# Two early pairs of layer 2, W_in's squares on GpSimd, and a new order table

## The chip, the cores and the metric

The kernel runs on one core of a Trainium2 chip. TensorE (PE in the rows) multiplies matrices into PSUM; VectorE (DVE), ScalarE (ACT) and GpSimd (POOL) do elementwise work; SyncE (SP) issues most of the DMAs between HBM and SBUF. Each engine runs its own list of instructions in order and waits for the others on semaphores. The metric is the time of one execution on the device, in microseconds (us). Of the kernel before, three runs are shown.

## The reference

Three parts follow one another: attention with rotary positions, a first feed-forward layer with a gate, and a second one with a rational activation. The 2304 tokens are 4 batches of 576.

```python
q_rot, k_rot = rotate(q), rotate(k)                      # 4 batches, 8 heads, 576 positions, 64 wide
scores = (1 / sqrt(64)) * q_rot @ k_rot^T
attn = exp(scores - max(scores))
attn = attn / (sum(attn) + 1e-09)
x = (attn @ v).transpose(0, 2, 1, 3).reshape(2304, 512)

h = x @ moe_w_in                                          # 512 -> 2048, layer 1
x = (h * clip(h + 3, 0, 6) / 6) @ moe_w_out               # 2048 -> 512

h = x @ moe2_w_in                                         # 512 -> 2048, layer 2
P = a0 + a1*h + a2*h^2 + a3*h^3
Q = 1 + |b0|*|h| + |b1|*h^2
out = (P / (Q + 1e-06)) @ moe2_w_out                      # 2048 -> 512
```

## The kernel before

All products run in 16 bit: a 32-bit matrix is scaled by a power of two and split into a high and a low half, and three matmuls (high by high, high by low, low by high) make one product. So every operand costs elementwise work: a copy to 16 bit for the high half, and a subtraction for the low one.

**Attention** goes by pairs of heads and batches. The rows q and k are loaded (`nat`), rotated by products with a table (lines 642 to 659), split (`ropea`, `gh`), and turned by a DMA transpose into `qkt`. TensorE makes the scores `s` (L706), VectorE their row maxima (L721), ScalarE the exponentials `e` (L738); `p` is their split (L760 is its low half), `pt` its transpose, and L796 the product with v. The scales of q, k and v come from totals over the partitions, which TensorE makes with ones (L455) from sums that ScalarE forms (`junk`, L444).

**Layer 1** runs in blocks of 256 tokens, two for each batch and a last one of what is left over; they start while later batches are still in attention. L901 is the first product (24 matmuls fill half a bank, two halves make one tile `h`); `t` is the activation, `gh` and `gl` its split (L315 or L313, L914), L929 the second product. Its result leaves PSUM as `t` (L313, L319) and goes by way of DRAM (`y1d`) to layer 2.

**Layer 2** runs in blocks of 512 tokens (five, the last of 256). Its first product makes two columns blocks of 128 features at a time, called a pair here: 24 matmuls at L1148 fill a PSUM tile, `hh` and `hx` in turn. Then six ScalarE and seven VectorE instructions (L1157 to L1173) make the activation and its split `lgh`, `lgl`, and 24 matmuls at L1183 add the pair to the four sums `ac`. A block has eight pairs. The tiles `lq`, `ls`, `lt`, `lr`, `lgh`, `lgl` are in a pool on the right side of SBUF, which starts where the tiles of layer 1 have been (line 998).

**Layer 2's weights** are loaded into a ring of three raw buffers (`raw2`), decoded to 32 bit (L424 to L429), and need a scale each before they can be split. For W_in the squares of all 16 tiles are summed over the partitions by TensorE (L1041, L511), for W_out ScalarE sums magnitudes (L444) and L455 makes the total; `w2ps` and `w2qs` (L403) are the scales. The split is one copy (L313, L315 or L319) and one subtraction (L1051) per tile (`w2i`, `w2o`).

**The order.** The kernel first writes down 3527 operations with what each reads and writes. The table ORDER then gives the order in which they are issued and, for those that may run on several engines, the engine; `order()` decodes it. So the order on each engine's list, and on SyncE's queue of DMAs, is what this table says. The dictionary PR holds, per kind of operation, on which engines it may run ('A' ScalarE, 'D' VectorE, 'G' GpSimd).

## Time and profile before

| what | value |
|---|---|
| median of 3 runs (lowest, highest) | 1084.6 us (1083.87, 1087.87) |
| the profiled execution | 1082.5 us, of which the span in the trace is 1080.7 |
| TensorE busy | 982.2 us (91%), granted clock 0.981 in the mean |
| VectorE busy | 905.7 us (84%), 1408 instructions |
| ScalarE busy | 780.5 us (72%), 1219 instructions |
| GpSimd busy | 61.2 us (6%), 71 instructions |

Matmuls overlap in the pipeline, so neighbours' times in the rows overlap as well. The granted clock is the share of full speed that TensorE was given: 1.00 is 2.4 GHz, and a stretch at the lower level is at 1.2 GHz. A share of busy time is an average over attention, layer 1 and layer 2, which have different limits.

### The profile page before, as it was taken

To read this page: it belongs to the slowest core of one execution; us is meant where nothing else is said; L and a number is where in the kernel's file an instruction comes from. 1 tells how busy PE (TensorE), PEld (TensorE's weight loads), DVE (VectorE), ACT (ScalarE), POOL (GpSimd) and SP (SyncE) were. 2 spreads that over 40 slices of the span, in tenths; PEclk is the share of its full clock that TensorE was granted. 3 is DMA by queue.
4 is the path that set the end of the run, shared out by engine and by line. 5 is a ranking of instruction groups with operands and counts; after the bars stand their busy time and mean duration, and the time that the engine had idled before them with its cause. 6 is when DMAs were issued, how large, how long until landed. Compare 5 with 4: busy or idle time off the path is not lost.

```text
span 1080.7 us, 20026 instructions
## 1 busy us (share of the span) xinstructions
PE 982.2 (91%) x7973; PEld 695.0 (64%) x7978; DVE 905.7 (84%) x1408; ACT 780.5 (72%) x1219; POOL 61.2 (6%) x71
## 2 busy tenths in 40 slices
...
GB/s 279 265 160 239 120 125 145 170 122 175 145 171 186 139 135 144 102 155 140 133 65 259 229 170 70 10 0 39 1 40 40 1 39 1 20 39 1 1 40 19
DMA packets 253853, 117.04 MB, mean 108 GB/s; under 512 B 223552, under 2 KB 241088, under 8 KB 253760
## 3 DMA queue, kind: packets, MB, share of 16 engines
...
## 4 chain that ended last, share of the span: by engine, by line
PE 63%; DVE 19%; ACT 9%; DMA 4%; issue 3%; POOL 1%; SPq 0%; ACTq 0%; DVEq 0%; POOLq 0%
PE ac L1183 13%; PE h L929 13%; PE h L901 10%; PE hh L1148 8%; PE hx L1148 7%; PE h L796 4%; PE s L706 3%; DVE mx L721 2%; DMA pt<-p 2%; DVE p L760 2%; DVE t L910 1%; DMA raw<-in_moe_w_in_dram 1%; PE h L787 1%; DVE lt L1163 1%; ACT e L738 1%
## 5 line engine op out<-in xcount | busy, mean ns | idle before, releaser
L901 PE MATMUL h<-xt,w 128*128 128x256 f16 x1728 | 199.7, 275 | 11.4 <-ACT xu L313 3.9
L901 PEld LDWEIGHTS <-w 128*128 128x128 f16 x1728 | 169.1, 99 | 33.6 <-issue 12.8
L929 PE MATMUL h<-gh,w 128*128 128x256 f16 x1080 | 190.3, 273 | 0.0
L929 PEld LDWEIGHTS <-w 128*128 128x128 f16 x1620 | 156.5, 98 | 18.8
L1183 PE MATMUL ac<-w2o,lgh 128*128 128x512 f16 x540 | 161.8, 382 | 3.3 <-ACT lgh L1172 3.3
L1148 PEld LDWEIGHTS <-w2i 128*128 128x128 f16 x900 | 89.1, 99 | 108.9 <-issue 24.0
L929 PE MATMUL h<-gl,w 128*128 128x256 f16 x540 | 147.2, 273 | 0.0
L738 ACT ACTIVATE e<-s,mx,qal 128x576 f32<-128x576 f32 (+1 forms) x144 | 114.5, 831 | 7.5 <-POOL mx L729 5.1
L1148 PE MATMUL hh<-x,w2i 128*128 128x512 f16 (+1 forms) x450 | 98.1, 365 | 8.5 <-ACT ls L1158 6.6
L1148 PE MATMUL hx<-x,w2i 128*128 128x512 f16 (+1 forms) x450 | 97.3, 364 | 6.7 <-ACT lq L1157 5.3
L1183 PE MATMUL ac<-w2o,lgl 128*128 128x512 f16 x270 | 102.8, 381 | 0.0
L721 DVE TENSOR_REDUCE mx<-s 128x2 f32<-128x1152 f32 (+1 forms) x80 | 99.1, 1242 | 3.7 <-PE s L709 3.2
L1183 PEld LDWEIGHTS <-lgh 128*128 128x128 f16 x576 | 56.5, 98 | 70.4 <-ACT lgh L1172 3.7
L760 DVE TENSOR_TENSOR p<-e,p 128x1152 f16<-128x1152 f32 (+1 forms) x72 | 89.2, 1239 | 11.3 <-ACT p L313 11.1
L1172 ACT ACTIVATE lgh<-lt 128x1024 f16<-128x1024 f32 (+1 forms) x40 | 38.6, 968 | 66.4 <-DVE lt L1171 43.8
L796 PE MATMUL h<-v,pt 128*128 128x130 f16 (+3 forms) x1440 | 77.4, 209 | 2.7 <-ACT xu L313 1.0
L908 ACT ACTIVATE t<-h,half,d 128x512 f32<-128x512 f32 (+1 forms) x96 | 61.6, 668 | 24.4 <-PE h L901 23.4
L796 PEld LDWEIGHTS <-pt 128*128 128x128 f16 (+1 forms) x1440 | 73.7, 102 | 7.3 <-issue 5.3
L313 ACT ACTIVATE p<-e 128x1152 f16<-128x1152 f32 (+1 forms) x61 | 64.3, 1054 | 12.1 <-DMA pt<-p 10.6
L706 PE MATMUL s<-qkt 64*128 64x512 f16 (+2 forms) x576 | 57.4, 326 | 8.8 <-ACT e L738 6.0
L1169 DVE SCALAR_TENSOR_TENSOR lt<-lt,cg,lr 128x1024 f32<-128x1024 f32 (+1 forms) x40 | 46.3, 1174 | 21.2 <-ACT lr L1167 21.2
L910 DVE SCALAR_TENSOR_TENSOR t<-t,h 128x512 f32<-128x512 f32 x72 | 48.9, 680 | 10.9 <-ACT t L908 10.4
...
## 6 DMA issues: line engine op xcount, KB each, us to landing
...
```

The source lines that it names most:

```text
L313: act.activation(out, in_, AF.Copy, scale=scale)
L706: pe.matmul(s()[:, a:b], lhsT=kq(1, y, 64 * h, 64 * h + 64)[:, cc * 128:cc * 128 + 128], rhs=kq(0, z, 64 * h, 64 * h + 64)[:, c:c + b - a] ...
L721: op("D", c_dve(n), lambda e: vec.reduce_max(mx()[:, 0, 0:g], sv().rearrange("p (g n) -> p g n", g=g), axis=AX.X, negate=True), r=[s], w=[ ...
L738: act.activation(et()[:, h * (n // g):(h + 1) * (n // g)], sv()[:, h * (n // g):(h + 1) * (n // g)], AF.Exp, bias=mx()[:, 1, h:h + 1], sca ...
L760: op(EN("lo"), c_sub(n), lambda e: EL[e].tensor_tensor(ph()[:, n:2 * n], et()[:, 0:n], ph()[:, 0:n], ALU.subtract), r=es + [(ph, 0)], w=[( ...
L796: pe.matmul(ob()[r0:r0 + m, o:o + k], lhsT=w, rhs=vv[:, 0:k], start=(z == 0 and j == 0), stop=(z == 1 and j == 4))
L901: pe.matmul(hp()[:, o:o + NQ], lhsT=wt[kk]()[:, z, c:c + 128], rhs=x, start=(n == 0), stop=(n == 11))
L908: act.activation(seg(t, c, n), seg(hp, c, n), AF.Relu, bias=half(), scale=x()[:, g:g + 1])
L910: op("D", c_dve(2 * NQ), lambda e, t=t, hp=hp: vec.scalar_tensor_tensor(t(), t(), two(-15), hp()[:, 0:2 * NQ], ALU.min, ALU.mult), r=[hp], ...
L929: pe.matmul(yp()[:, o:o + NQ], lhsT=w[:, s_, m_ * 128:(m_ + 1) * 128], rhs=gt()[:, f], start=(f == 0 and z == 0), stop=(f == KF - 1 and z ...
L1148: pe.matmul(hp()[:, x * n:x * n + n], lhsT=wi[kk]()[:, z, c:c + 128], rhs=xt()[:, kk, y, 0:n], start=(i == 0), stop=(i == 11))
L1183: pe.matmul(accs[j][i]()[0:m], lhsT=gt()[:, y * n + x:y * n + x + m], rhs=wt, start=(f == 0 and z == 0), stop=(f == KF - 1 and z == 2))
```

## The change

Three things are changed.

- Layer 2's first two pairs of block 0 (`l2e` = 2) both use the PSUM tile `hh`, and their elementwise tiles come from the left pool: the three `raw2` buffers take the place of `lq`, `lt`, `ls` and `lr` (the last two share one), and the tile `y1`, through which layer 2's inputs pass, takes that of `lgh` and `lgl`.
- The 16 squares of W_in may run on GpSimd, as a tensor_tensor product, instead of a ScalarE activation; the high half of the split of layer 2's weights may run on GpSimd too.
- The table ORDER is another one. 279 of the 3527 operations change their engine. By operations, GpSimd has 161 instead of 67, VectorE 1386 instead of 1405, ScalarE 1015 instead of 1078, TensorE 678 as before; 12 DMA issues move from SyncE's queue to ScalarE's. GpSimd now has all 16 squares, 14 low halves of layer 1's activation (`gl`), 9 low halves and 9 high halves of `p`, 13 of the rotation's products and sums, 23 scalings of row maxima (16 before), and 18 high halves of layer 2's weights.

```diff
--- before.py
+++ after.py
@@ -61,7 +61,8 @@
  'e_vl': 'D',
  'e_vl0': 'D',
  'e_w': 'A',
- 'e_w2h': 'A',
+ 'e_w2h': 'GA',
+ 'e_w2q': 'G',
  'e_wl': 'D',
  'e_wl0': 'D',
  'e_xh': 'G',
@@ -69,6 +70,7 @@
  'e_y': 'AD',
  'e_y0': 'D',
  'f32': 1,
+ 'l2e': 2,
  'lo': 'D',
  'lo0': 'D',
  'ns': 4,
@@ -91,73 +93,69 @@
  'x2f': 8}
 
 ORDER = (
-    'c-qx@flnMudgoWw(>*iYJ;Q)mc9!QQ1o2ox5FxV!5so015Dsw`=Ou_(gkuSdSmbjMOAvWM4rlo|uf=l2LWuY{mRKB%Sb_*a9A^>YI0SJ##34V9',
...
+    'c-lo+4NP3wbw2m~&6_umnK8>c6BfCI5K3J{kxLxpP95qZLMU>OMcomllu+UzmpW)m9cmGauBd|?>Jp2k1R<BY6N_$;LtR9Xi!5XjLR@OiTErz5',
...
 )
 
 
@@ -1038,8 +1036,12 @@
             bound((w2am, f), lambda: w2am()[:, f:f + 1], w2f[wi, f], 512)
         else:
             z = (f % KD, f // KD % 2)
-            op("A", c_act(512), lambda e: act.activation(sqs()[:, z[0], z[1]].bitcast(BF16), w2f[wi, f](), AF.Square), r=[w2f[wi, f]],
-               w=[(sqs, z)])
+            def sq(e, x=w2f[wi, f]):
+                if e == "A":
+                    act.activation(sqs()[:, z[0], z[1]].bitcast(BF16), x(), AF.Square)
+                else:
+                    EL[e].tensor_tensor(sqs()[:, z[0], z[1]].bitcast(BF16), x(), x(), ALU.mult)
+            op(PR["e_w2q"], {"A": c_act(512), "D": c_dve(512), "G": c_pool(512)}, sq, r=[w2f[wi, f]], w=[(sqs, z)], share=True)
             if f % KD == KD - 1:
                 norm_w2(f // KD)
 
@@ -1135,7 +1137,8 @@
         t0, n = blocks[j]
         xt = x2s[j]
         cf, dv, cg = coef[j]
-        i_ = f // 2 % 2
+        first = j == 0 and f < 2 * PR["l2e"]
+        i_ = 0 if first else f // 2 % 2
         hp = tl("ps3", [128, 2 * N2], F32, "hx", 1) if i_ else tl("ps2", [128, 2 * N2], F32, "hh", 1)
         wi = w2[0][f // KD * KD:f // KD * KD + KD]
         n2 = 2 * n
@@ -1149,11 +1152,28 @@
                                   stop=(i == 11))
                         i += 1
             op("P", c_pe(n, 12), mm, r=[xt] + wi, w=[(hp, x)])
-        q, sq, t, rr = t2("lq", 2), t2("ls", 2), t2("lt", 3), t2("lr", 2)
-        gh, gl = t2("lgh", 3, F16), t2("lgl", 3, F16)
-
-        def s(t_):
-            return t_()[:, 0:n2]
+        if first:
+            q, t, sq = [tl("p2", [128, 512, 2], I32, "raw2", PR["raw2"]) for _ in range(3)]
+            rr = sq
+            if f == 0:
+                x2s["g"] = tl("p2", [128, KD, N2], F32, "y1", 1)
+            gx = x2s["g"]
+            gkey = [(gx, f), (gx, f + 1)]
+
+            def s(t_):
+                return t_().rearrange("p n two -> p (n two)").bitcast(F32) if t_ is not hp else t_()[:, 0:n2]
+
+            def g(i):
+                return gx()[:, (f + i) % KD].bitcast(F16)
+        else:
+            q, sq, t, rr = t2("lq", 2), t2("ls", 2), t2("lt", 3), t2("lr", 2)
+            gkey = [t2("lgh", 3, F16), t2("lgl", 3, F16)]
+
+            def s(t_):
+                return t_()[:, 0:n2]
+
+            def g(i):
+                return gkey[i]()[:, 0:n2]
         op("A", l2_act(n2, 1, False), lambda e: act.activation(s(q), s(hp), AF.Abs, scale=cf()[:, 0:1]), r=[hp, cf], w=[q])
         op("A", l2_act(n2, 1, False), lambda e: act.activation(s(sq), s(hp), AF.Square, scale=dv()[:, 0:1]), r=[hp, dv], w=[sq])
         op("A", l2_act(n2, 2, False), lambda e: act.activation(s(t), s(hp), AF.Identity, bias=cg()[:, 2:3], scale=cg()[:, 3:4]),
@@ -1169,8 +1189,8 @@
         op("D", l2_dve(n2, 1), lambda e: vec.scalar_tensor_tensor(s(t), s(t), cg()[:, 0:1], s(rr), ALU.add, ALU.mult),
            r=[rr, (cg, 0)], w=[t])
         op("D", l2_dve(n2), lambda e: vec.scalar_tensor_tensor(s(t), s(q), -2.0, s(t), ALU.add, ALU.mult), r=[q], w=[t])
-        op("A", l2_act(n2), lambda e: act.activation(s(gh), s(t), AF.Copy), r=[t], w=[gh])
-        op("D", l2_dve(n2), lambda e: vec.tensor_tensor(s(gl), s(t), s(gh), ALU.subtract), r=[t, gh], w=[gl])
+        op("A", l2_act(n2), lambda e: act.activation(g(0), s(t), AF.Copy), r=[t], w=[gkey[0]])
+        op("D", l2_dve(n2), lambda e: vec.tensor_tensor(g(1), s(t), g(0), ALU.subtract), r=[t, gkey[0]], w=[gkey[1]])
         nt = [(x, min(128, n - x)) for x in range(0, n, 128)]
         if f == 0:
             accs[j] = [tl("ps2", [128, DM], F32, f"ac{i}") for i in range(len(nt))]
@@ -1179,14 +1199,14 @@
 
             def mo(e, nt_=tuple(enumerate(nt)), y=y, wo=wo, f=f + y):
                 for i, (x, m) in nt_:
-                    for z, (gt, wt) in enumerate(((gh, wo()[:, 0]), (gh, wo()[:, 1]), (gl, wo()[:, 0]))):
-                        pe.matmul(accs[j][i]()[0:m], lhsT=gt()[:, y * n + x:y * n + x + m], rhs=wt, start=(f == 0 and z == 0),
+                    for z, (gt, wt) in enumerate(((0, wo()[:, 0]), (0, wo()[:, 1]), (1, wo()[:, 0]))):
+                        pe.matmul(accs[j][i]()[0:m], lhsT=g(gt)[:, y * n + x:y * n + x + m], rhs=wt, start=(f == 0 and z == 0),
                                   stop=(f == KF - 1 and z == 2))
             if 0 < f + y < KF - 1:
-                op("P", c_pe(DM, 3 * len(nt)), mo, r=[gh, gl, wo], w=accs[j])
+                op("P", c_pe(DM, 3 * len(nt)), mo, r=gkey + [wo], w=accs[j])
             else:
                 for i, x in enumerate(nt):
-                    op("P", c_pe(DM, 3), lambda e, i=i, x=x, mo=mo: mo(e, ((i, x),)), r=[gh, gl, wo], w=[accs[j][i]])
+                    op("P", c_pe(DM, 3), lambda e, i=i, x=x, mo=mo: mo(e, ((i, x),)), r=gkey + [wo], w=[accs[j][i]])
         if f == KF - 2:
             for i, (x, m) in enumerate(nt):
                 ob = tl("p2r", [128, DM], F32, "ob", PR["ob"])
```

The rows below stand as the program is issued: number, line, instruction, result and operands. A line of the changed kernel is up to 2 lower than the same line of before, and 20 higher in layer 2's elementwise part.

VectorE, at the end of layer 1 and around the scale of W_out (`w2qi`, `w2qv`, `w2qs`; L319 or L317 is the last result of layer 1 leaving PSUM). Before:

```order
952 L521 TENSOR_REDUCE w2am<-w2am 128x1
953 L397 TENSOR_SCALAR w2qi<-h_75 128x1
954 L401 TENSOR_SCALAR w2qv<-w2qi 128x1
955 L403 RECIPROCAL w2qs<-w2qv 128x1
956 L1109 TENSOR_TENSOR cg<-gu,w2qv 128x1
957 L1051 SCALAR_TENSOR_TENSOR w2i_9170<-w2o_8364,w2qs,w2i_9170 128x512
958 L1051 SCALAR_TENSOR_TENSOR w2o_9185<-w2o_8407,w2qs,w2o_9185 128x512
959 L319 TENSOR_SCALAR t<-h_76,d 128x2x64 x4
960 L1051 SCALAR_TENSOR_TENSOR w2o_9200<-w2o_8484,w2qs,w2o_9200 128x512
961 L1051 SCALAR_TENSOR_TENSOR w2o_9209<-w2o_8466,w2qs,w2o_9209 128x512
962 L1051 SCALAR_TENSOR_TENSOR w2o_9212<-w2o_8521,w2qs,w2o_9212 128x512
963 L319 TENSOR_SCALAR w2o_9238<-w2o_8584,w2qs 128x512
964 L1163 TENSOR_TENSOR lt<-lt,hh 128x1024
965 L1051 SCALAR_TENSOR_TENSOR w2o_9238<-w2o_8584,w2qs,w2o_9238 128x512
966 L1164 SCALAR_TENSOR_TENSOR lt<-lt,cg,hh 128x1024
```

After:

```order
940 L1183 TENSOR_TENSOR raw_8980<-raw_8980,hh 128x1024
941 L1181 SCALAR_TENSOR_TENSOR raw_8974<-raw_8982,kc,raw_8974 128x1024
942 L317 TENSOR_SCALAR t<-h_76,d 128x2x64 x4
943 L519 TENSOR_REDUCE w2am<-w2am 128x1
944 L395 TENSOR_SCALAR w2qi<-h_76 128x1
945 L1184 SCALAR_TENSOR_TENSOR raw_8980<-raw_8980,cg,hh 128x1024
946 L1188 SCALAR_TENSOR_TENSOR raw_8974<-raw_8974,raw_8982 128x1024
947 L399 TENSOR_SCALAR w2qv<-w2qi 128x1
948 L401 RECIPROCAL w2qs<-w2qv 128x1
949 L1189 SCALAR_TENSOR_TENSOR raw_8980<-raw_8980,cg,raw_8982 128x1024
950 L317 TENSOR_SCALAR w2i_9140<-w2o_8406,w2qs 128x512
951 L1053 SCALAR_TENSOR_TENSOR w2i_9140<-w2o_8406,w2qs,w2i_9140 128x512
952 L1191 SCALAR_TENSOR_TENSOR raw_8980<-raw_8974,raw_8980 128x1024
953 L1053 SCALAR_TENSOR_TENSOR w2o_9144<-w2o_8418,w2qs,w2o_9144 128x512
```

The elementwise work of pair 0 (`raw_8974`, `raw_8980`, `raw_8982` and `hh`) stood behind nine rows of W_out's splits; now it begins ahead of layer 1's last result and goes on between the instructions of the scale.

The squares of W_in (`x` from `w2i`), on ScalarE before:

```order
622 L426 ACTIVATE raw_8203<-raw_8203,down 128x512
623 L424 ACTIVATE w2i_8277<-raw_8203 128x512
624 L426 ACTIVATE raw_8221<-raw_8221,down 128x512
625 L1041 ACTIVATE x_7902<-w2i_8134 128x512
626 L424 ACTIVATE w2i_8298<-raw_8221 128x512
627 L1041 ACTIVATE x_7902<-w2i_8169 128x512
628 L1041 ACTIVATE x_7902<-w2i_8200 128x512
629 L1041 ACTIVATE x_7902<-w2i_8236 128x512
630 L426 ACTIVATE raw_8262<-raw_8262,down 128x512
631 L424 ACTIVATE w2i_8323<-raw_8262 128x512
632 L1041 ACTIVATE x_7902<-w2i_8277 128x512
633 L1041 ACTIVATE x_7902<-w2i_8298 128x512
```

and on GpSimd after:

```order
108 L758 TENSOR_TENSOR p_7479<-e,p_7479 128x640
109 L912 TENSOR_TENSOR gl<-t,gh 128x512 x2
110 L1043 TENSOR_TENSOR x_7955<-w2i_7797 128x512
111 L1043 TENSOR_TENSOR x_7955<-w2i_7933 128x512
112 L1043 TENSOR_TENSOR x_7955<-w2i_7906 128x512
113 L1043 TENSOR_TENSOR x_7955<-w2i_7965 128x512
114 L313 TENSOR_SCALAR gh<-t 128x512
115 L1043 TENSOR_TENSOR x_7955<-w2i_7938 128x512
116 L1043 TENSOR_TENSOR x_7955<-w2i_8031 128x512
117 L1043 TENSOR_TENSOR x_7955<-w2i_8038 128x512
118 L912 TENSOR_TENSOR gl<-t,gh 128x512
119 L313 TENSOR_SCALAR gh<-t 128x512
```

They stood between the decoding of the weights; now they stand in GpSimd's list with layer 1's casts `gh` and subtractions `gl`.

SyncE at the start of attention, where the two DMA transposes of the first pair of heads are issued. Before:

```order
27 L412 DMA raw<-in_moe_w_in_dram 128x1024
28 L677 DMA_TRANSPOSE qkt<-ropea 128x10x128
29 L615 DMA nat_83<-in_k_dram 128x2x256
30 L618 DMA nat_83<-in_k_dram 64x64 x2
31 L412 DMA raw<-in_moe_w_in_dram 128x1024 x2
32 L615 DMA nat_83<-in_q_dram 128x2x256
33 L618 DMA nat_83<-in_q_dram 64x64 x2
34 L677 DMA_TRANSPOSE qkt<-ropea 128x10x128
```

After:

```order
27 L616 DMA nat_130<-in_k_dram 64x64 x2
28 L613 DMA nat_130<-in_q_dram 128x2x256
29 L616 DMA nat_130<-in_q_dram 64x64 x2
30 L675 DMA_TRANSPOSE qkt<-ropea 128x10x128
31 L410 DMA raw<-in_moe_w_in_dram 128x1024
32 L675 DMA_TRANSPOSE qkt<-ropea 128x10x128
33 L410 DMA raw<-in_moe_w_in_dram 128x1024 x3
```

The loads that were queued between the two transposes now stand ahead of the first or behind the second, but for one.

## Rows read from the trace of the kernel before

**Rows 1.** Which engine the chain of waits ran through: the page's fourth part.

```profile
PE 63%; DVE 19%; ACT 9%; DMA 4%; issue 3%; POOL 1%; SPq 0%; ACTq 0%; DVEq 0%; POOLq 0%
```

**Rows 2.** Busy time by stage: from:to, length, busy (instructions) of each engine, granted clock, DMA.

```profile
0.00:100.00 100.00, 52.26 (x289) 45.48 (x290) 83.89 (x180) 88.02 (x192) 9.60 (x13) 0.97 0.83 233
300.00:400.00 100.00, 98.06 (x1122) 84.36 (x1120) 93.32 (x152) 70.97 (x112) 14.07 (x16) 1.00 0.81 160
653.90:675.20 21.30, 21.28 (x196) 18.84 (x194) 8.43 (x17) 12.07 (x30) 0.00 (x0) 1.00 0.27 88
675.20:731.00 55.80, 42.32 (x169) 17.68 (x171) 49.13 (x54) 42.77 (x47) 0.00 (x0) 0.88 0.02 5
```

**Rows 3.** TensorE in order of time: start, length, instruction, idle time before and releaser.

```profile
674.91 0.27 PE L929 MATMUL h<-gh,w 128*128 128x256 f16 x1
676.40 0.39 PE L1148 MATMUL hx<-x,w2is 128*128 128x512 f16 x1 [1.22 <-DVE t L319]
...
686.40 8.16 PE L1148 MATMUL hh<-x,w2i 128*128 128x512 f16 x24 [4.65 <-ACT ls L1158]
695.00 5.35 PE L1148 MATMUL hx<-x,w2i 128*128 128x512 f16 x24 [0.43 <-DVE lt L1164]
702.20 5.34 PE L1148 MATMUL hh<-x,w2i 128*128 128x512 f16 x24 [1.85 <-ACT lq L1157]
...
718.07 7.70 PE L1148 MATMUL hx<-x,w2i 128*128 128x512 f16 x24 [5.35 <-ACT lq L1157]
725.60 0.59 PE L1183 MATMUL ac<-w2o,lgh 128*128 128x512 f16 x2
...
730.57 0.38 PE L1183 MATMUL ac<-w2o,lgl 128*128 128x512 f16 x1
```

**Rows 4.** The same view of TensorE, layer 2's first pair.

```profile
650.65 0.81 PE L1148 MATMUL hh<-x,w2i 128*128 128x512 f16 x3
```

**Rows 5.** The same view of ScalarE, the first pair's first elementwise instruction.

```profile
679.21 1.19 ACT L1159 ACTIVATE lt<-hh,cg 128x1024 f32<-128x1024 f32 x1
```

**Rows 6.** The same view of VectorE, the scale of W_out.

```profile
671.26 0.16 DVE L397 TENSOR_SCALAR w2qi<-h 128x1 int32<-128x1 int32 x1 [6.81 <-PE h L455]
```

**Rows 7.** The squares of W_in: durations (min/median/max), first and last start.

```profile
L1041 ACT ACTIVATE x<-w2i x16: 611/615/643, 570.2 to 609.5; 128x512 bf16<-128x512 f32 x16
```

**Rows 8.** GpSimd by group: instructions, busy us and mean ns, idle before.

```profile
L315 POOL TENSOR_SCALAR gh<-t 128x512 f16<-128x512 f32 x25 | 26.0, 1039 | 268.8 <-DVE t L910 224.7 <-DVE gu L1096 39.4 <-DVE gu L1104 4.7
```

**Rows 9.** GpSimd in order of time, one kind of cast at three places.

```profile
140.75 0.62 POOL L315 TENSOR_SCALAR gh<-t 128x512 f16<-128x512 f32 x1 [3.53 <-DVE t L910]
...
635.38 1.75 POOL L315 TENSOR_SCALAR gh<-t 128x512 f16<-128x512 f32 x1 [0.26 <-DVE t L910]
640.77 0.79 POOL L315 TENSOR_SCALAR gh<-t 128x512 f16<-128x512 f32 x1 [3.64 <-DVE t L910]
```

**Rows 10.** VectorE in order of time, one instruction at two places.

```profile
641.12 0.98 DVE L1051 SCALAR_TENSOR_TENSOR w2i<-w2i,w2ps,w2i 128x512 f16<-128x512 f32 x1
...
656.65 0.74 DVE L1051 SCALAR_TENSOR_TENSOR w2i<-w2i,w2ps,w2i 128x512 f16<-128x512 f32 x1
```

**Rows 11.** VectorE by group, of the kinds that GpSimd takes over.

```profile
L760 DVE TENSOR_TENSOR p<-e,p 128x1152 f16<-128x1152 f32 x56 | 75.7, 1351 | 9.6 <-ACT p L313 9.5
L914 DVE TENSOR_TENSOR gl<-t,gh 128x512 f16<-128x512 f32 x72 | 49.2, 684 | 6.2 <-ACT gh L313 3.0 <-POOL gh L315 3.0
...
L1171 DVE SCALAR_TENSOR_TENSOR lt<-lq,lt 128x1024 f32<-128x1024 f32 x32 | 38.4, 1218 | 0.1
...
L642 DVE TENSOR_TENSOR ropea<-nat,tab 128x640 f32<-128x640 f32 x28 | 22.3, 815 | 2.6 <-DMA nat<-in_q_dram 2.6
```

**Rows 12.** SyncE's DMA issues at the start.

```profile
27.46 2.40 SPq L677 DMA_TRANSPOSE qkt<-ropea  x1
...
35.66 1.92 SPq L677 DMA_TRANSPOSE qkt<-ropea  x1
```

**Rows 13.** TensorE at the start, the last total ahead of the first scores.

```profile
42.43 0.59 PE L455 MATMUL h<-qam,ones 128*128 128x3 f32 x2 [9.63 <-ACT junk L444]
```

More of the change, by code (lines that the diff above doesn't have):

```diff
@@ new lines @@
+    'Y#7?087(a;&8*HES1O%6X9YmftqOcygll+5EyUyw76%@&r>w)Af|GLCibJ0ghA`Y>IyA7ya6L2QLC;M?R}&rnC{q&|smk6~GMO-}5W{!YG*~{o',
+    'PXqjv<`X4ky{$}|ZO2xVXBfA<gSM{FUX01S>FBr3Z<t@8aVTWFAo&~2MWrs-^)r<WD>Io5xu48rbQtsK(3vsh0_$2%o2BE*7jip<@q9~W9^LY^',
+    'LWxz$W|fo~%|v7!7RZcNYK{ms5QM6P!G=5qF#G1<hheBqmw6gJy=LL@=?`M6!2;|D=G&f1HUXgo?vc~wK6b8Vx|9&~(;aqE4O<cUu@#e}iTj=%',
+    'L_;Y%X*va=kEYlNJW7XQ($g)UIo7d1lo|2O*cSqo9}dGKyG446+5MjUM`_&}dSgAgAqC;CwIhdM$FCpMS(~_eC>>)48$guZ&l#}%aGQ-CkN#p9',
+    '&!%I1>gB=U$j@5*W4LEUV3w^OL>b_DXW=vK^MR>@+bo3WDX|KGX9nJEiN6T+#dYX2NAv1nKHeTUb1?6Z9`wQ(>xFu=1K&B`>Y$Hlp9sMZ_C81M',
@@ new lines @@
+    'vr^3U*O+L95YLllgX~B2&k#RMu;b9fc5|vQCOSMeLvNnJNb2z3hxu^*c-}7xJ(tZbsl^V%bJ+)<3YNw@OdZCRyO{ZD#E}kn^ZMyUw8qyvAC0|H',
+    'dbq*X#Jb(QV7I9&EpW-af(SdK38_ok6MNI7-g<}Mdr#!=A0^-N8AhYFkkp|9cFPOj*EGxCqLN(<v))Kb(F{C)CV5ZOpf&jrzqKS&n#wk89cIK{',
+    '$iSX;URX^V@}eAsdc&jmpi8_;rdbzkTS56g-hW()%FPh8b|oDy(FWlJU4dR0g*xL4%D;*2P8j{@G2`A{`z*xGN4iDpK{w`owTQb7`IPn81pS3u',
+    '>gd+GHzxeZ&4FEe(yUN=l@|8gtxUBk@0l^L29>E>dNV6BhV|=*psXnGntv#**tL=$RAmd#H!ro&+LRw!l>#MUHYx4qj#;8KDP=Te7b`p(Bj&ho',
+    '-rTi1klQAe-vA%PL|#YNVO{C8VzkhX@+fB}lyWfSCTp3^df(aCU`#vhybzzuL;F+-niKlpSw5)uTGkySt_*k`>zQZgP?86&h#6P<B}rE8GS60q',
```

118 lines of the change are left out of this document (52 added, 66 removed).

## The prediction

> **What bounds the kernel now.** I read the chain of waits first: 63% of it is TensorE, 19% VectorE, 9% ScalarE [rows 1]. So an edit pays where TensorE stands still or runs at its lower clock. The table by stage then says where that is [rows 2]. In the middle of attention (300 to 400 us) TensorE is busy 98.06 of 100 us, with VectorE at 93.32 right behind it: little to win, something to lose. In the first 100 us TensorE is busy only 52.26 while ScalarE (88.02) and VectorE (83.89) do the preparation: those two are the limit there. From 675.2 to 731 us TensorE is busy 42.32 of 55.80 us at a granted clock of 0.88: this is the start of layer 2.
>
> The timeline of TensorE at that start [rows 3] is the heart of the matter. Layer 1's last matmul ends at 674.91 + 0.27 = 675.2 us, and the second product of layer 2's pair 1 (pairs counted from 0) ends at 730.57 + 0.38 = 730.95. Between them lie the first products of five pairs and the second products of two. Their price at the full clock is 5.35 us each (the row at 695.00; 725.60 to 730.95 for a second product), so 7 x 5.35 = 37.4 us of work takes 55.8 us. The missing 18.4 us are five gaps, 1.22 + 4.65 + 0.43 + 1.85 + 5.35 = 13.5 us, and two groups at the lower clock, (8.16 - 5.35) + (7.70 - 5.35) = 5.2 us, each right behind a gap of over 4 us. The cause stands earlier: pair 0's first product is finished by 651.5 us [rows 4], but ScalarE first reads it at 679.21 [rows 5], since its result tiles lie in the memory that layer 1's tiles still hold. Meanwhile VectorE is busy 8.43 of the 21.30 us in which TensorE runs layer 1's last products, ScalarE 12.07 [rows 2], and VectorE sits still for 6.81 us ahead of W_out's scale [rows 6]. After that everything comes at once: W_out's splits and the elementwise work of pairs 0 and 1, 49.13 us of VectorE's work in 55.80 us.
>
> **The first two pairs (l2e).** Removed: the wait for layer 1's tiles, as pairs 0 and 1 write into the three raw buffers and the y1 buffer instead. No instruction is added. Pair 0's elementwise work is seven VectorE instructions of the kind that takes 1.22 us [rows 11], 8.5 us, and six ScalarE ones of up to 1.19 [rows 5] with one table load, some 8 us. In the new order they stand ahead of and around W_out's scale, in the 21.3 us where the two engines have 12.9 and 9.2 us free, so they fit. Behind layer 1's end the same 37.4 us of matmuls remain, and two limits. By TensorE: I find by the order one short gap, about 1.7 us, for the low part of pair 0's result behind ScalarE's and VectorE's splits, so 39.1 us, a gain of 16.7. By VectorE: 49.1 - 8.5 = 40.6 us of its work plus some 1.5 us until its first input, so 42.1 us, a gain of 13.7. I take 15. The bounds: all 18.4 us go, or only the first two gaps with their slow group (1.22 + 4.65 + 2.81 = 8.7) while VectorE makes the 5.35 us gap again. The y1 buffer now is free later, for block 1's inputs; block 0 has eight pairs of 10.7 us, so that is covered. The three raw buffers are shared with W_out's last loads; if pair 0 had to wait for those the low bound would hold.
>
> **W_in's squares on GpSimd.** Removed from ScalarE: 16 x 0.615 = 9.8 us, spread over 570 to 610 us [rows 7]. ScalarE isn't the limit there, so by itself this frees nothing on the path. On GpSimd the new order puts 16 squares, 3 casts and 4 subtractions in one row. The trace has no tensor_tensor on GpSimd; the nearest row is its 128x512 cast, 1.04 us in the mean [rows 8], and single ones took 0.62 to 1.75 [rows 9]. At the mean the chain is 23 x 1.04 = 24 us, at 1.75 it is 40: the old window is 39 us long, so it just fits at the high end. I take 0, with 9 us of delay to W_in's scale if each took twice the mean (48 us).
>
> **About 94 more operations on GpSimd.** By the rows of before, some 28 us leave VectorE and 48 us ScalarE: 9 subtractions p (five wide ones of 1.35 us, four of 640 columns at about 0.8), 14 of gl at 0.68, 13 rope products and sums at about 0.82 [rows 11], casts, maxima and splits. What GpSimd costs the others the trace shows in part. The same cast took 0.62 us at one place and 1.75 at another [rows 9]. One started at 640.77 and lasted 0.79; VectorE's instruction at 641.12 with two inputs in SBUF then took 0.98 us, where 0.74 is its time without such company [rows 10]: 0.24 us. The Trainium skill says more, in "SBUF — State Buffer", section "SBUF: two separate sides": a VectorE instruction with two SBUF inputs and a GpSimd instruction that reads SBUF lock each other out for the whole of the instruction that came first. By that rule the 0.24 us is the tail of the lock, as 640.77 + 0.79 is behind 641.12, and the trace agrees. At 0.24 us each, 94 operations cost VectorE 23 us of the 28 it was relieved of. Bounds: nothing lost (28 us of relief, of which at 98% TensorE little can be cashed, some 4 us), or VectorE held through each long one (the last rival). I take +3, as the new products are longer than that cast and more of each is likely to be met.
>
> **The prologue.** The second transpose of pair 0 was issued at 35.66, 8.2 us behind the first [rows 12], with loads queued between; now one load stands between, so it can go at about 31. TensorE however began on the scores only behind a total for which it waited 9.63 us on ScalarE [rows 13]; the new order puts two groups of scores ahead of it. Since VectorE and ScalarE limit this stage, I count what leaves VectorE there: three rope products and sums of about 0.82 and two casts that are shorter, some 3.5 us. I take -3; bounds +4 (GpSimd's longer products come late for the transposes) and -10 (the 9.63 us wait goes).
>
> **Before the transition and the tail.** Between W_in's scale and pair 0's first product the new order gives VectorE a little more to do than TensorE, as the old one did: 0, bounds 5 both ways. The last pairs have the same instructions in a slightly other order: 0, bounds 2.
>
> **Sum.** -15 - 3 + 3 = -15 us. The profiled execution took 1082.5 us (span 1080.7 and 1.8 around it), so 1067.5; the median of the runs is 2.1 higher, so 1069.6, put down as 1069.
>
> **Rivals.**
> 1. VectorE bounds the transition, or pair 0 waits for the raw buffers: for it speak 49.13 busy of 55.80 us; against it that 8.5 us of this move ahead. Gain 8.7: -8.7, about 1076.
> 2. The squares come late: for it the chain that fits only up to 1.75 us each; against it the mean of 1.04. The scale of W_in is 9 us late: -6, about 1078.5. The Trainium skill speaks for it: "GPSIMD Engine Reference", section 3.1, has GpSimd at about half of VectorE's speed in elementwise work. By that, with VectorE's 0.68 us for a 128x512 product, one takes about 1.4 us and the chain 32 us, an estimate that still fits; no row here shows it.
> 3. Slower: VectorE is held by GpSimd's two-input instructions in attention. Some 30 of them (p, rope, half of gl) took VectorE 26 us; at twice that on GpSimd, 53 us, with VectorE held throughout, it loses 27 us more than it gained, in a stage where it is busy 93 of 100 us and TensorE 98. Then TensorE waits for about 26 us: -15 - 3 + 26 = +8, about 1092. For it speak the 1.75 us cast and the 0.98 us row; against it that only 0.24 us were lost there, and that PSUM reads, such as the row maxima, are not among the instructions held. It decides once VectorE loses over half of GpSimd's time.
> 4. The prologue's wait goes whole and the relief counts in attention: -15 - 10 = -25, about 1059.
>
> **Numbers.** Forecast 0.54 (own range 1062 to 1074), rival 1 0.16, rival 2 0.09, rival 3 0.12, rival 4 0.09. Faster by over 0.5% means under 1079.2, slower over 1090.0; less than 0.5% (5.4 us) a measurement of this kernel can't well tell from no change. Faster: 0.54 + 0.16 + 0.09 and a little over half of rival 2's 0.09, less a small part of the first two that may lie above, 0.80. Same: 0.10, from the rest of these and a weaker rival 3. Slower: 0.10, most of rival 3. The range 1056 to 1085 leaves out most of rival 3 and the best of rival 4.
>
> **What would show it.** ScalarE's first instruction on pair 0's product about 15 us or more ahead of layer 1's last matmul; TensorE's span from there to the second product of pair 1 near 40 us, at clock 1.00. Wrong would be: a gap over 4 us behind layer 1's end with VectorE as releaser; W_in's scale behind the last square on GpSimd; VectorE's two-input instructions in attention longer by over half of GpSimd's time, and TensorE under 96 of 100 us there.

## The result and the profile after

The changed kernel takes 1069.44 us in the median of four runs (1068.87 to 1070.27), the one before 1084.24 (1083.87 to 1087.87): the ratio is 0.9836, with a 95% interval of 0.9809 to 0.9863. The forecast was 1069. The profiled execution took 1069.65 us with a span of 1067.9, so 12.8 us less than the 1080.7 of before. In the experiments further on the runs of one kernel lie up to 9 us apart, so differences of a few us are taken from medians and from the profiles, at equal work done by TensorE: the columns that its matmuls stream are added up in the order in which the matmuls end, and the times at which two kernels reach the same sum are compared. Where nothing else is said the comparison is with the first profile of the changed kernel, and a place is named by the time in that profile.

Busy time by stage of the changed kernel, in the columns of [rows 2] (from:to, length, then busy and instructions of PE, PEld, DVE, ACT, POOL, the granted clock, DMA):

```profile
0.00:100.00 100.00, 45.02 (x268) 37.92 (x269) 85.30 (x179) 86.33 (x187) 15.79 (x18) 0.91 0.84 239
100.00:600.00 500.00, 480.72 (x5282) 411.44 (x5282) 431.80 (x694) 334.96 (x545) 130.40 (x113) 0.99 0.65 146
653.90:675.40 21.50, 21.50 (x199) 19.25 (x198) 15.25 (x27) 16.46 (x29) 2.43 (x3) 1.00 0.12 42
675.40:715.40 40.00, 37.06 (x169) 15.98 (x166) 33.09 (x37) 23.35 (x28) 12.04 (x8) 1.00 0.10 33
715.40:908.50 193.10, 183.00 (x843) 82.11 (x843) 167.29 (x199) 133.96 (x142) 1.08 (x1) 1.00 0.07 22
908.50:1062.50 154.00, 153.59 (x807) 78.64 (x805) 129.01 (x172) 98.65 (x125) 0.00 (x0) 1.00 0.05 18
```

The same for the kernel before, in the stages that [rows 2] does not have:

```profile
100.00:600.00 500.00, 479.70 (x5282) 412.03 (x5282) 432.80 (x708) 361.19 (x595) 45.29 (x52) 0.99 0.75 149
731.00:924.40 193.40, 191.81 (x886) 86.86 (x888) 166.42 (x203) 127.80 (x135) 0.00 (x0) 1.00 0.08 25
924.40:1074.70 150.30, 145.14 (x760) 74.31 (x758) 121.46 (x159) 97.40 (x119) 0.00 (x0) 0.99 0.04 15
```

Layer 1 ends at 675.4 us, 0.2 later than before: at that point nothing has been won. From there the kernel needs 387.1 us to its last matmul at 1062.5, the one before needed 399.5 (675.2 to 1074.7). TensorE's idle time tells where the 12.4 us are. To 715.4 us it is 2.9 us, where before 13.5 were idle up to 731 and another 5.2 lost to the lower clock. To 908.5 it is 10.1, before 1.6. In the last blocks it is 0.4, before 5.2.

TensorE in order of time at the start of layer 2 (as [rows 3]):

```profile
675.24 0.38 PE L1151 MATMUL hh<-x,w2is 128*128 128x512 f16 x1
...
681.92 0.39 PE L1203 MATMUL ac<-w2i,y 128*128 128x512 f16 x1 [0.90 <-DVE y L1193]
...
689.53 5.35 PE L1151 MATMUL hh<-x,w2i 128*128 128x512 f16 x24
694.72 8.13 PE L1203 MATMUL ac<-w2o,y 128*128 128x512 f16 x36
704.19 2.75 PE L1151 MATMUL hh<-x,w2i 128*128 128x512 f16 x12 [1.34 <-ACT lq L1177]
707.52 2.75 PE L1151 MATMUL hx<-x,w2i 128*128 128x512 f16 x12 [0.58 <-DVE lt L1184]
...
712.69 2.75 PE L1151 MATMUL hx<-x,w2i 128*128 128x512 f16 x12
...
725.25 5.35 PE L1151 MATMUL hx<-x,w2i 128*128 128x512 f16 x24 [2.72 <-DVE lt L1184]
```

Pair 1's first product starts right behind layer 1, and at 712.69 + 2.75 = 715.4 us the same seven groups are done for which the kernel before took until 730.95: 40.0 us instead of 55.8. The gaps in it are 0.90, 1.34 and 0.58 us, and no group is at the lower clock. The 2.72 us at 725.25 are already the next stage. ScalarE's first instruction on pair 0's product, and the casts to the high half of pairs 0 and 1:

```profile
660.40 1.10 ACT L1177 ACTIVATE raw<-hh,cf 128x1024 f32<-128x1024 f32 x1
...
676.29 1.06 ACT L1192 ACTIVATE y<-raw 128x1024 f16<-128x1024 f32 x1 [5.05 <-DVE raw L1191]
...
694.90 1.06 ACT L1192 ACTIVATE y<-raw 128x1024 f16<-128x1024 f32 x1 [5.13 <-DVE raw L1191]
```

The first stands at 660.40 us, 15.0 us ahead of layer 1's end. The kernel before got to it at 679.21 [rows 5], behind layer 1's end.

All engines, from the page:

```profile
PE 971.1 (91%) x7978; PEld 686.2 (64%) x7978; DVE 908.9 (85%) x1389; ACT 738.2 (69%) x1144; POOL 186.2 (17%) x165
```

GpSimd is busy for 125 us more and ScalarE for 42 less (it had 780.5). VectorE is busy for 908.9 us where it was 905.7, with 19 instructions fewer. What GpSimd's new work takes, by group (as [rows 8]):

```profile
L1043 POOL TENSOR_TENSOR x<-w2i 128x512 bf16<-128x512 f32 x16 | 19.4, 1231 | 26.1 <-DVE qb L1019 13.0 <-DVE up L1022 7.7 <-DVE w2i L427 5.4
L912 POOL TENSOR_TENSOR gl<-t,gh 128x512 f16<-128x512 f32 x14 | 19.2, 1370 | 39.7 <-ACT gh L311 26.2 <-DVE r L842 8.8 <-ACT w2i L422 3.2
...
L313 POOL TENSOR_SCALAR w2o<-w2o,w2qs 128x512 f16<-128x512 f32 x8 | 13.3, 1660 | 45.4 <-DVE w2o L1053 28.0 <-DVE w2i L1053 17.4
L758 POOL TENSOR_TENSOR p<-e,p 128x1152 f16<-128x1152 f32 x5 | 11.9, 2373 | 35.3 <-DVE p L315 18.4 <-ACT p L311 12.0 <-DMA nat<-in_q_dram 4.9
L657 POOL TENSOR_TENSOR rot<-nat,ropea 128x640 f32<-128x640 f32 x6 | 10.7, 1789 | 31.0 <-DVE nat L647 31.0
L640 POOL TENSOR_TENSOR ropea<-nat,tab 128x640 f32<-128x640 f32 x5 | 10.4, 2077 | 10.2 <-DMA qkt<-ropea 10.2
```

A square is 1.04 us in the median (the mean of 1.23 has some slower ones), a wide p 2.37, a rotation product 2.08 where VectorE takes 0.815 [rows 11]. The other side of it is on VectorE:

```profile
L912 DVE TENSOR_TENSOR gl<-t,gh 128x512 f16<-128x512 f32 x58 | 43.3, 753 | 3.1 <-POOL gh L313 1.7 <-ACT gh L311 1.4
...
L1053 DVE SCALAR_TENSOR_TENSOR w2i<-w2i,w2ps,w2i 128x512 f16<-128x512 f32 x15 | 12.8, 856 | 0.5 <-POOL w2i L313 0.2
```

and of the last line before:

```profile
L1051 DVE SCALAR_TENSOR_TENSOR w2i<-w2i,w2ps,w2i 128x512 f16<-128x512 f32 x15 | 11.9, 793 | 1.9 <-ACT w2i L313 1.7
```

The 58 subtractions gl that it kept take 0.753 us instead of 0.684 [rows 11], and the subtractions of W_in's split 0.856 instead of 0.793.

### The profile page after: what moved, and what is told of

Read it like the earlier page. It is cut to its first block, busy times and chain, and to the rows that moved or that the text cites. A ratio compares the mean times of both kernels' runs of the same rounds, so it can differ in the third digit from the quotient of the medians.

```text
span 1067.9 us, 20042 instructions
## 1 busy us (share of the span) xinstructions
PE 971.1 (91%) x7978; PEld 686.2 (64%) x7978; DVE 908.9 (85%) x1389; ACT 738.2 (69%) x1144; POOL 186.2 (17%) x165
## 4 chain that ended last, share of the span: by engine, by line
PE 41%; DVE 15%; ACT 7%; issue 3%; POOL 1%; ACTq 0%; DVEq 0%; POOLq 0%
PE h L927 10%; PE ac L1203 10%; PE h L899 8%; PE hx L1151 4%; PE hh L1151 4%; PE h L794 3%; DVE lt L1183 2%; PE s L704 1%; DVE lt L1184 1%; DVE lq L1188 1%; DVE lt L1189 1%; DVE lt L1191 1%; DVE lgl L1193 1%; ACT ls L1178 1%; ACT lq L1177 1%
## 5 line engine op out<-in xcount | busy, mean ns | idle before, releaser
L1203 PE MATMUL ac<-w2o,lgh 128*128 128x512 f16 x516 | 153.4, 379 | 0.5 <-ACT lgh L1192 0.5
L736 ACT ACTIVATE e<-s,mx,qal 128x576 f32<-128x576 f32 (+1 forms) x144 | 115.7, 831 | 14.8 <-POOL mx L727 6.1
L1151 PE MATMUL hh<-x,w2i 128*128 128x512 f16 (+1 forms) x468 | 100.3, 359 | 2.8 <-DVE y1m L1083 1.4
L1203 PE MATMUL ac<-w2o,lgl 128*128 128x512 f16 x258 | 97.8, 379 | 1.1 <-DVE lgl L1193 1.1
L1151 PE MATMUL hx<-x,w2i 128*128 128x512 f16 (+1 forms) x432 | 91.0, 357 | 6.3 <-DVE lt L1184 3.3
L1203 PEld LDWEIGHTS <-lgh 128*128 128x128 f16 x544 | 53.1, 98 | 64.0 <-issue 1.2
L906 ACT ACTIVATE t<-h,half,d 128x512 f32<-128x512 f32 (+1 forms) x96 | 61.5, 667 | 43.1 <-PE h L899 33.1
L758 DVE TENSOR_TENSOR p<-e,p 128x1152 f16<-128x1152 f32 (+1 forms) x63 | 79.8, 1267 | 7.2 <-ACT p L311 6.1
L311 ACT ACTIVATE p<-e 128x1152 f16<-128x1152 f32 (+1 forms) x53 | 58.0, 1093 | 3.0 <-DMA pt<-p 1.4
L424 ACT ACTIVATE raw<-raw,down 128x512 int32<-128x512 uint16 x64 | 48.1, 758 | 14.1 <-DMA raw<-in_moe_w_in_dram 11.4
L1181 DVE SCALAR_TENSOR_TENSOR lq<-ls,kc,lq 128x1024 f32<-128x1024 f32 (+1 forms) x38 | 44.3, 1168 | 12.8 <-ACT lq L1177 9.4
```

Of the source, the lines that this page charges most:

```text
L311: act.activation(out, in_, AF.Copy, scale=scale)
L736: act.activation(et()[:, h * (n // g):(h + 1) * (n // g)], sv()[:, h * (n // g):(h + 1) * (n // g)], AF.Exp, bias=mx()[:, 1, h:h + 1], sca ...
L758: op(EN("lo"), c_sub(n), lambda e: EL[e].tensor_tensor(ph()[:, n:2 * n], et()[:, 0:n], ph()[:, 0:n], ALU.subtract), r=es + [(ph, 0)], w=[( ...
L906: act.activation(seg(t, c, n), seg(hp, c, n), AF.Relu, bias=half(), scale=x()[:, g:g + 1])
L1151: pe.matmul(hp()[:, x * n:x * n + n], lhsT=wi[kk]()[:, z, c:c + 128], rhs=xt()[:, kk, y, 0:n], start=(i == 0), stop=(i == 11))
L1203: pe.matmul(accs[j][i]()[0:m], lhsT=g(gt)[:, y * n + x:y * n + x + m], rhs=wt, start=(f == 0 and z == 0), stop=(f == KF - 1 and z == 2))
```

## The experiments

All are the changed kernel with another order or other engines for some operations. Where the order is another one, operations whose inputs, buffers or banks are not free at their place are put off until they are; that happened in the first experiment alone. The edits are shown in short. The runs were made on two chips, so each time stands with its ratio to the kernel before on the same chip; an interval that overlaps that of the changed kernel does not tell the two apart by itself.

**The pairs without the early tiles.** Pairs 0 and 1 on right-pool tiles, as before.

```diff
- 'l2e': 2,
+ 'l2e': 0,
```

> The changed kernel with its own table, but layer 2's pairs 0 and 1 again on the tiles of the right pool and on the PSUM tiles hh and hx in turn; the 57 operations that the table issues before these tiles are free are put off until they can go. Theory T (the early pairs fill the gaps behind layer 1's end, 18.7 us lost there before and 7.1 after): 9 to 13 us of the gain go, 1078 to 1083 us, and ScalarE's first instruction on pair 0's product stands behind layer 1's last matmul again. Rival R (the new order of W_out's scale and splits made the gain, the tiles don't matter): 1069 to 1073 us.

Measured: 1084.13 us, ratio to before 0.9974 (0.9957 to 0.9991), where the changed kernel has 0.9836 to 0.9861. TensorE and ScalarE at the same place:

```profile
674.93 0.38 PE L1212 MATMUL hx<-x,w2is 128*128 128x512 f16 x1 [1.23 <-ACT t L372]
...
688.16 1.03 PE L1264 MATMUL ac<-w2i,lgh 128*128 128x512 f16 x2 [7.90 <-ACT lgh L1253]
...
696.35 6.94 PE L1212 MATMUL hx<-x,w2i 128*128 128x512 f16 x24 [2.96 <-DVE lt L1245]
```

```profile
675.36 1.13 ACT L1238 ACTIVATE lq<-hh,cf 128x1024 f32<-128x1024 f32 x1
```

The gap is back, as one of 7.90 us and one of 2.96, with a group at the lower clock behind it (6.94 instead of 5.35), and ScalarE's first instruction stands at 675.36. At equal work it is 1.7 us ahead of the changed kernel at layer 1's end, 13.6 behind at 690 us, and 13.0 behind at the end. Theory T holds (its range is 1078 to 1083 us; with the first 1084.24 us for the kernel before, the ratio gives 1081): without the early tiles the new order does not make the gain. What the tiles would give with the old order was not run.

**The first cut: the front of before, up to 560 us.** The first 2169 operations in the order and on the engines of before, then the rest as the changed table has it.

```diff
+        seq = old[:2169] + [x for x in new if x[0] not in have]   # have: the operations of old[:2169]
```

> All operations that the kernel before issues up to about 560 us of its trace, in its order and on its engines, then the rest as the changed kernel has it. At equal work done the changed kernel is 2.6 us behind there. Theory T (nothing is won in attention; the gain is made in layer 2 alone): 1067 us, 1065 to 1069. Rival R (the new front prepares the transition, by relief of VectorE and ScalarE, and is part of the gain): 1072 us or more.

Measured: 1078.98 us, ratio 0.9942 (0.9918 to 0.9966). By the time alone the rival would hold, but at equal work the kernel is 0.8 us ahead at 569 us and 6.0 behind at 592. TensorE has one wait in between:

```profile
582.71 1.65 PE L1033 MATMUL h<-xt,w 128*128 128x256 f16 x7 [4.24 <-DVE t L1042]
```

Ahead of it ScalarE waited 3.00 us for a load of W_in, where it waits 1.06 in the changed kernel. So the loss is at the cut; that the cut made the load late is likely and not shown. The run doesn't decide; it was made again with another cut (below).

**The end in the order of before,** from 895 us.

```diff
+        seq = new[:3087] + [x for x in old if x[0] not in have]
```

> The changed kernel up to about 895 us of its trace, and from there all that is left in the order of the kernel before. Between that point and the end the changed kernel was 5.8 us faster. Theory T (the order of the last pairs makes these 5.8 us by itself): 1074 to 1076 us. Rival R (they are the wake of an earlier lead, since VectorE catches up): 1069 to 1071 us.

Measured: 1081.78 us, ratio 0.9949 (0.9931 to 0.9968). The time is above both forecasts. At equal work it loses 3.8 us between 895 and 905, 2.0 more to 1000, and 6.3 from 1050 to the end. TensorE's longest wait there, before and in this run:

```profile
PE ac L1183 <- ACT lgh L1172: 3.3, 1, 3.3
PE ac L1337 <- ACT lgh L1326: 3.3, 1, 3.3
```

The wait of the last pairs comes back with the old order, and from 1060 to 1076 us the clock is 0.79 in the mean. So what theory T says of the last pairs holds, and rival R falls; the 3.8 us at the cut were in neither.

**GpSimd's new work back: all, VectorE's part, ScalarE's part.** Only the engine changes, the order stays.

```diff
+        seq = [[i, was[i] if k < end and e == "G" else e, b] for k, (i, e, b) in enumerate(new)]
+        # g_back_dve: ... and was[i] == "D";  g_back_act: ... and was[i] == "A"
```

> The changed kernel with its order, but the 85 operations ahead of W_in's squares that it moved to GpSimd go back to the engines that had them before, 43 to ScalarE and 42 to VectorE (row maxima, casts gh and gl, splits of p, rotation). Theory T (VectorE gets back 26 us of work and loses some 25 us of waiting for GpSimd): within 3 us, 1066 to 1072. Rival A (the relief counts): 1075 or more. Rival B (the mutual waiting of VectorE and GpSimd costs more than the relief is worth): 1065 or less.

Measured: 1091.69 us, ratio 1.0046 (1.0024 to 1.0068): slower than the kernel before. Rival A holds and theory T falls, so the 85 operations were parted by the engine that had them.

> Of the 85 operations that the run before put back (19 us slower in its profile), only the 42 that VectorE had go back from GpSimd to VectorE: low halves of p and gl, the rotation, some casts. Theory T (VectorE's relief is eaten up by its waiting for GpSimd: its busy time stayed at 906 to 909 us though 28 us of work left it; what counts is ScalarE's relief): within 4 us of the changed kernel, ratio to before 0.980 to 0.988. Rival (VectorE's relief counts, busy time hides it): 10 us or more slower than the changed kernel, ratio 0.993 or more.

Measured: 1072.09 us, ratio 0.9882 (0.9850 to 0.9915), 2.9 us above the changed kernel that was run beside it (1069.17, further below). The two intervals overlap, so this run is not clear of no change; the 10 us of the rival are excluded. Theory T holds.

> The other 43 of the 85 go back from GpSimd to ScalarE: scalings of row maxima, casts gh, high halves of p and of layer 1's weights. Theory T (ScalarE's relief counts): 12 us or more slower than the changed kernel, ratio to before 0.995 or more. Rival (VectorE's relief counts): within 4 us of the changed kernel, ratio 0.980 to 0.988.

Measured: 1088.80 us, ratio 1.0020 (1.0001 to 1.0039), 19.6 us above it: theory T's number holds. The busy times from the pages, VectorE's part back and ScalarE's part back:

```profile
PE 983.4 (91%) x7972; PEld 697.0 (65%) x7978; DVE 919.3 (85%) x1431; ACT 739.6 (69%) x1144; POOL 123.2 (11%) x123
```

```profile
PE 977.9 (90%) x7972; PEld 689.2 (63%) x7978; DVE 901.6 (83%) x1389; ACT 760.0 (70%) x1187; POOL 147.4 (14%) x122
```

With its 42 operations back, some 26 us of work by the rows of before, VectorE is busy for 919.3 us, only 10.4 more than in the changed kernel: the other 16 us GpSimd had cost it in longer instructions. So the relief of VectorE is worth little, 2.9 us or less. ScalarE's 43 operations are 21.8 us of its time (760.0 for 738.2) and cost 19.6 us of the whole. VectorE is busy for 901.6 us with them back, 7.3 less than in the changed kernel, though its own work is the same. ScalarE's list is in order, and the maxima's scaling and the casts stand in front of what TensorE waits for. TensorE and a stage of this kernel:

```profile
384.07 0.39 PE L587 MATMUL h<-qam,ones 128*128 128x3 f32 x2 [1.45 <-ACT xu L445]
386.23 1.15 PE L838 MATMUL s<-qkt 64*128 64x512 f16 x5 [1.77 <-ACT e L870]
```

```profile
384.00:400.00 16.00, 14.16 (x137) 11.47 (x137) 10.00 (x23) 10.29 (x17) 2.43 (x1) 0.79 0.67 136
```

There are two waits of 1.45 and 1.77 us for ScalarE, and the clock is 0.79 in the mean of these 16 us. At equal work this kernel falls from 4 to 15 us behind between 300 and 400 us: TensorE is idle for 8.9 us there instead of 2.4, and the clock is 0.95 instead of 1.00. ScalarE itself waits longer in this stretch for the maxima that it now scales (the changed kernel first, then this one):

```profile
ACT mx L725 <- DVE mx L719: 3.6, 3, 2.7
ACT mx L859 <- DVE mx L853: 9.6, 6, 4.9
```

So the 19.6 us are the price of these operations at the places of an order that was made without them. They are not the price of ScalarE's load: the kernel before has the 43 operations on ScalarE too, in an order of its own, and is as fast up to layer 1's end (0.2 us).

**The squares back on ScalarE.**

```diff
+        seq = [[i, "A" if self.ops[i].nm == ">x2" and self.ops[i].engs == "G" else e, b] for i, e, b in new]
```

> The changed kernel with W_in's 16 squares on ScalarE again, at the same places of the order. Theory T (off the path: ScalarE has 40 of 100 us free at 500 to 600 us): within 2 us of the changed kernel, W_in's scale not later. Rival (the squares held up ScalarE's decoding of the weights or the layer 1 evictions): 5 us or more slower. Rival 2 (GpSimd's squares cost VectorE, which waited 4 us for them): 3 us faster.

Measured: 1074.23 us, ratio 0.9894 (0.9859 to 0.9930), 5.1 us above the changed kernel; the intervals overlap, so it is the profile that has to decide. In front of the squares it is 3.0 us behind, which is of the first 130 us, and after them 7.6: 4.6 us are lost at the squares, so theory T falls. The stage, and TensorE's longest wait there:

```profile
580.00:600.00 20.00, 18.37 (x166) 16.03 (x165) 12.98 (x27) 18.02 (x33) 1.81 (x3) 1.00 0.57 183
```

```profile
621.47 1.04 PE L570 MATMUL h<-x,ones 128*128 128x512 bf16 x3 [1.68 <-DVE t L378]
...
624.09 1.02 PE L570 MATMUL h<-x,ones 128*128 128x512 bf16 x4 [0.28 <-DVE w2cm L572]
```

TensorE waits 1.68 us for an eviction ahead of the third sum of squares (`h` from `x` and `ones`). The fourth and last one starts at 624.09 and ends 1.0 us later, at 625.1; in the changed kernel the last one ends at 617.8. Over the whole stretch (563 to 649.6 us here, 560 to 642 in the changed kernel) TensorE is idle for 8.4 us instead of 4.5, each time for a VectorE instruction, most often the second one of layer 1's activation (`t`), which waits for ScalarE's first. Changed kernel, then this run:

```profile
DVE t L908 <- ACT t L906: 2.7, 3, 2.0
DVE t L969 <- ACT t L967: 5.5, 7, 1.2
```

So the squares held up ScalarE's part of layer 1, as the rival says. ScalarE is busy 18.0 of 20 us here, where its share of the 100 us from 500 is 60. In the changed kernel it has 16.9 of the same 20 us, and before, with the squares, 17.9, so the share alone does not tell what a microsecond of work costs.

> The changed kernel once more, on the same chip as the three others, to compare them with: ratio to before 0.982 to 0.987, as measured first. If this chip shows another ratio, the experiments are read against this one.

Measured: 1069.17 us (1066.83 to 1076.04), ratio 0.9854 (0.9819 to 0.9889).

**The front of before up to 595 us, the later pairs of before, and both.** The cuts lie where the second order expects nothing that the first has not yet done, on the side where that is possible.

```diff
+        # front595:  old[:2298], then new
+        # steady_before:  new[:2830], old[:3101], new
+        # both:  old[:2298], new[:2830], old[:3101], new
```

> The order and the engines of the kernel before up to about 595 us, then the changed table. The first try cut at 560 us, where the changed table had already done work on layer 2's weights that the old one does later; its trace lost 6.9 us in one stall at that seam and was 0.8 us ahead in front of it. Here nothing is left behind at the cut. Theory T (the two fronts are equal, the offload to GpSimd only pays for the new order's other placing): ratio to the changed kernel 0.997 to 1.002, thus 1066 to 1071 us where that takes 1069. Rival (the changed front prepares layer 2's start): 1073 us or more.

Measured: 1075.67 us, ratio 0.9893 (0.9865 to 0.9921), where the changed kernel beside it has 1072.85 and 0.9861; the intervals overlap. At equal work it is 0.5 us ahead at 540 us, 1.8 behind at layer 1's end and 3.3 from 730 us on. Neither theory is met by the time. From 570 to 620, in the preparation of layer 2, it loses 2.4 us. The other 1.5 us are not the front's, as the next run shows, which has the changed kernel's order up to 774 us and loses the same 1.5 us at the same place:

```profile
724.59 6.91 PE L1286 MATMUL hx<-x,w2i 128*128 128x512 f16 x24 [2.72 <-DVE lt L1319]
```

The changed kernel has the same wait at 725.25, and the group behind it takes 5.35 us at the full clock. In six of the thirteen profiles that have this wait the group takes 6.8 to 7.0 us, in the others 5.35, and the order does not decide which.

> The changed kernel, but from about 774 to 889 us of its trace the order of the kernel before, in blocks 0 and 1 of layer 2. There TensorE waits for 4.8 us in the changed kernel and for 1.0 in the one before. Theory T (what is won at layer 2's start is partly given back by the new order of the later pairs): 3 to 4 us faster than the changed kernel, some 1065.5 us. Rival (TensorE, having come forward, now meets VectorE's limit whatever the order): within 1.5 us of the changed kernel.

Measured: 1075.16 us, ratio 0.9885 (0.9854 to 0.9917), 2.3 above the changed kernel; the intervals overlap. At equal work it is 0.9 us behind at 774, loses 2.2 at the first cut, gains 5.2 from 800 to 895, as the kernel before does there, and loses 5.3 behind the second cut. TensorE is idle for 3.0 us from 774 to 895 instead of 4.8, and for 4.0 from 895 to 990 instead of none. Neither forecast is met: between the cuts the old order does have fewer waits, and as much is lost again behind them. How much of that the cuts themselves cost is not shown.

> Both edits of the two kernels ahead together. Theory T: the sum of the two effects within 2 us, at best 1064 us and faster than either kernel. Rival (the seams cost what the pieces save): 1069 us or more.

Measured: 1077.52 us, ratio 0.9909 (0.9881 to 0.9937). The two losses add up (2.8 and 2.3 us, together 4.7), but theory T's 1064 us is far off, and by the time the rival holds. No mixture beats the changed kernel.

> The changed kernel once more, on the same chip as the three others and only to compare them with: ratio to before 0.982 to 0.987.

Measured: 1072.85 us (1066.76 to 1075.54), ratio 0.9861 (0.9829 to 0.9893).

## Why the prediction was right, point by point

**The sum** was -15 us and is -12.8 in the profiled executions, -14.8 in the medians. Its main term holds in mechanism and size. The rest was forecast at 0 and came to +3. That it is no more is luck: the terms for the prologue and for GpSimd missed, the later pairs were left out, and the misses made up for each other.

- **The start of layer 2, -15:** right. 55.8 us became 40.0, -15.8; the two limits given were 39.1 and 42.1. It was TensorE's limit that held, with 37.06 us busy and three short gaps; VectorE, for which 40.6 us of work were counted, is busy for 33.1 of the 40. The experiment without the early tiles lost 13.0 us of it.
- **The later pairs, not in the sum:** missed. TensorE is idle for 10.1 us between 715.4 and 908.5, where before it was 1.6. Its largest waits there:

```profile
PE hx L1151 <- DVE lt L1184: 2.7, 1, 2.7
PE hx L1151 <- ACT ls L1178: 1.6, 1, 1.6
PE hh L1151 <- DVE y1m L1083: 1.4, 1, 1.4
PE hh L1081 <- DVE lt L1184: 1.3, 1, 1.3
```

The largest is for VectorE's instruction that gives the first product's PSUM tile free. So VectorE is late, as rival 1 had it, but only behind the transition; that it is late because TensorE has come forward and W_out's splits have not become fewer is argued and not shown. With the old order from 774 to 889 us the waits between the cuts were fewer, but the kernel was not faster, so whether the order has a part in it stays open.

- **The tail, 0 with bounds of 2:** missed by 5 us in favour. The 3.3 us wait of the last `ac` for ScalarE was in the waits of before, and the new order avoids it. Together with the later pairs it comes to +3.4.
- **The prologue, -3:** wrong in sign. TensorE starts on the scores earlier, at 39.6 instead of 43.0 us, but is busy only 45.02 of the first 100 us instead of 52.26 [rows 2], at a clock of 0.91 instead of 0.97. At equal work the changed kernel is 6.3 us behind the one before at 100 us and 7.6 at 130. It is 3.1 behind at 150, 1.2 at 250, 1 to 4.5 behind up to 620, and level at 640.
- **GpSimd, +3:** not a loss behind the prologue, since what the prologue lost is made up by layer 1's end; which part of that is GpSimd's and which the order's was not told apart. Right that VectorE's relief is spent on longer instructions, and by more than the 23 of 28 us that I took. On balance it was not relieved of 28 us: it gave 98 operations away and took 79 over, and by its instructions in the two traces, at the mean durations of before, that is 22.7 us less. Its busy time rose by 3.2 us, so it lost some 26. The experiments show where: with them back VectorE's instructions are shorter by some 16 us for the 42 operations that came from VectorE, by 7.3 for the 43 that came from ScalarE, and by 3.8 for the 16 squares (905.1 us busy with those on ScalarE).
- **ScalarE's relief, at nothing:** open for the 48 us as a whole. The 43 operations put back cost 19.6 us in this order, but the kernel before, with that load and its own order, is as fast up to layer 1's end. For the squares, "ScalarE isn't the limit there, so by itself this frees nothing on the path" was too little: put back they cost 4.6 us in the profile, and from 560 to 640 us the kernel before, with an order of its own for them, loses 2.4 us to the changed one.
- **Attention together, 0 by -3 and +3:** 0.2 us at layer 1's end, right as a sum only.
- **The rivals:** the squares did not delay layer 2. They take 1.04 us each in the median and the last one ends at 613.8, the sums of squares at 617.8 instead of 611.7, but layer 2's first product starts at 641.1 us, before at 640.9. VectorE was held in attention as the third rival said (its two-input instructions there take 1.4 to 2.4 us on GpSimd, 1.8 to 2.6 times VectorE's time), but it lost about what it was relieved of, not 27 us more, and TensorE stayed at 480.7 of 500 us (479.7 before).

The Trainium skill's rule on the lock ("SBUF — State Buffer", section "SBUF: two separate sides") goes with these runs, which show longer instructions and not the lock itself: with 42 of GpSimd's operations back on VectorE, VectorE's other instructions got some 16 us shorter. The pair of rows that the prediction used for it shows less than the rule says: the two instructions overlap for 0.44 us (641.12 to 641.56), and VectorE's was 0.24 us longer [rows 9], [rows 10]. The Trainium skill's statement that GpSimd has about half of VectorE's speed ("GPSIMD Engine Reference", section 3.1, "Elementwise — side-by-side cycle accounting") agrees for the wide p, 2.37 us to 1.35, 1.8 times as long; a rotation product took 2.08 to 0.815, 2.6 times, and the rows do not tell how much of that is waiting for VectorE.

What stays open: what ScalarE's lighter load is worth by itself, since the kernel with the new order and that load back had no order made for it.
